# Half of the pairs write their quotient as two float32r parts and multiply w_out in three float32r products; PSUM tiles are handed on in halves

## The chip, the cores and the metric

The kernel runs on one core of a Trainium2 chip. The core has a matrix engine (PE, with its weight loads shown apart as PEld), three engines for elementwise work (DVE, ACT, POOL) and a queue that starts transfers (SP). The metric is the device time of one execution in microseconds; less is better. A time is given as the median of the runs of one kernel, and the traces come from one profiled execution.

## What is computed

A channel attention for four batches, and then a feed-forward layer whose activation is a rational function. Cut to what matters:

```
qn = q / (norm(q, axis=1) + 1e-6)            # q, k, v: 4 x 6080 x 256
kn = k / (norm(k, axis=1) + 1e-6)
s  = kn.transpose(0, 2, 1) @ qn / tau        # 4 x 256 x 256
a  = exp(s - s.max(-1)); a /= a.sum(-1) + 1e-9
x  = (v @ a).reshape(24320, 256)
h  = x @ w_in                                # w_in: 256 x 2048
P  = a0 + a1*h + a2*h^2 + a3*h^3
Q  = 1 + |b0|*|h| + |b1|*h^2
out = (P / (Q + 1e-6)) @ w_out               # w_out: 2048 x 256
```

## The kernel before

**Tiling.** The rows are cut in groups of 512 (the last group of each batch has 448), 12 groups to a batch and 48 in all. The 2048 columns of the hidden layer are cut in eight *pairs* of 2 x 128 columns, so there are 384 units of work, each a pair `p` (0 to 7) of a group. The attention matrix is multiplied into `w_in` once a batch (`fuse`), so that a pair is one product of the value rows with a fused weight. That product is taken in three float32r products of high and low parts: `vhi`, `vlo` and the two halves of a `w` tile (`mm1`, 12 matmuls of 512 columns).

**One pair** (`pair`, L598 to L675). `mm1` writes a tile `hx` of two PSUM banks. Then 1024 values per partition run through the elementwise engines: ACT, DVE and POOL make the denominator `d`. In the plain form ACT squares, POOL multiplies and adds one (`line`), ACT takes the absolute value and POOL adds (`sum`). In the *factored* form (`p` in 1, 3, 6, from the second group on) ACT takes an absolute value, DVE multiplies (`prod`), ACT takes the absolute value again, and POOL adds one (`one`). ACT and DVE make the numerator (`slope`, `num1`, `num2`), which is written over `hx`. ACT takes the reciprocal square root of `d` and squares it, which gives a first reciprocal `r` (`root`, `square`). A Newton step mends it: POOL multiplies `d` by `r` (`again`), DVE forms the quotient with `r` (`quot`) and corrects it into a tile `g` (`last`). `mm2` multiplies `g` by the float32 `w_out_sb` into `acc`, the one accumulator of the group, also two PSUM banks; each of its 8 matmuls stands as two in the trace. After the eight pairs, `finish` copies `acc` to `orow` and stores it.

**Beside the pairs.** While a batch runs, the next batch's scores are gathered (`Attn`: loads of `kq`, squares on ACT, sums `ssq` on POOL, products on PE, `sacc` on DVE). Each weight piece of 512 columns arrives as raw words in a `raw` buffer and is put together by six DVE operations with a `work` tile of its own (`piece`, L302 to L373). Twelve pieces are *early*: their `work` tiles lie in PSUM (`acc` or `hx`). The last four of `w_out` work in the SBUF tiles `cv` and `cv2`.

**What sets the order.** Every operation is a `step` with an engine, a cost and a key. `Planner.order` (L111) runs a list of these steps through a model of the engines, and takes on each engine the ready step with the lowest key whose buffers are free. The keys come from the tables `LAG` and `TIME`. The result is one fixed order per engine; on the chip the engines only wait for each other's semaphores. A buffer tag has a fixed number of slots (`SLOTS`): three `hx` tiles of two PSUM banks, one `acc`, four `d`, four `uu`, three `r`, four `g`.

All operations are recorded by one helper (L43), so the profile is read by tiles and not by lines.

Of the kernel before, what the change touches and what calls it, by code (L numbers as in the profile page):

```python
# [21 lines left out]
    "first": 2.42, "prod": 2.04, "abs": -4.64, "line": 9.56, "second": 3.75, "sum": -23.6, "slope": 5.71,  # L22
    "num1": 23.17, "num2": 21.53, "root": 8.83, "one": -1.7, "square": -3.23, "again": 5.54, "quot": 8.31,
    "last": 10.3, "out": 23.21,
}
TIME = {
    "pair": 3.57, "start": 48.71, "load": 1.9, "softmax": 48.77, "in": 5, "late_in": 3.83, "out0": 2.3,
    "out": 5.39, "attn0_0": -0.02, "attn_0": 0.98, "attn0": 3.82, "attn": 2.42, "attn1": 91.81, "value": 3.3,
    "fuse": 1.77, "finish": 10.12, "front": 45.32, "front_pace": 2.4,
# [20 lines left out]
class Buf:  # L50


    def __init__(self, tag=None, view=None):
        self.tag, self.view = tag, view
        self.tile, self.slot = None, None
        self.writers, self.readers = [], []
        self.left = 0
        self.owner, self.until = None, 0.0

# [8 lines left out]
class Planner:  # L68
# [10 lines left out]
    def add(self, eng, cost, key, fn, reads=(), writes=(), port=False):  # L79
# [20 lines left out]
        for b in {id(b): b for b in (*reads, *writes)}.values():  # L100
            if b.tag is not None:
                b.left += 1
                s.bufs.append(b)
# [7 lines left out]
    def order(self):  # L111
# [17 lines left out]

        def fits(s):  # L130
            want = {}
# [8 lines left out]
        while left:  # L140
            for e in ready:
                while busy[e] <= now and ready[e]:
# [9 lines left out]
                    if pick is None:  # L152
                        break
                    for b in pick.new:
                        b.slot = free[b.tag].pop(0)
# [36 lines left out]
def tile_channel_attention_rational_ffn(  # L192
# [25 lines left out]
    while n0 < N:  # L218
# [8 lines left out]
    FACTORED = (1, 3, 6)  # L227
# [11 lines left out]
    SLOTS = {"hx": 3, "acc": 1, "d": 4, "uu": 4, "r": 3, "g": 4, "w": 10, "kq": 4, "sq": 2, "ssq": 1,  # L239
             "vst": 1, "vhi": 2, "vlo": 2, "orow": 2, "sacc": 1, "eT": 1, "cv": 1, "cv2": 1, "n2": 1,  # L240
             "s0": 1, "y": 1, "e": 1, "sm": 1}
    plan = Planner(SLOTS, ("d", "uu", "r", "g", "w", "kq", "sq", "cv", "cv2", "vst", "vhi", "vlo", "orow", "acc"), ("hx", "acc"))
# [6 lines left out]

    def buf(tag, shape, dtype=F32, name=None):  # L250


        def view(slot):
            sizes = dict(zip("abc", shape[1:]))
            t = homes[tag][slot]
# [6 lines left out]
        homes.setdefault(tag, 0)  # L262
        homes[tag] = max(homes[tag], math.prod(shape[1:]))
        return Buf(tag, view)

    def step(eng, cost, key, fn, reads=(), writes=(), port=False):
# [7 lines left out]
        plan.add(eng, cost, key, run, reads, writes, port)  # L274
# [16 lines left out]
    b0, b1 = babs[:, 0:1], babs[:, 1:2]  # L291
    w_in_sb = const.tile([P, NC2, F], F32, name="w_in_sb")
    w_out_sb = const.tile([P, NF, C], F32, name="w_out_sb")

# [7 lines left out]
    def piece(side, m, at, c):  # L302
# [9 lines left out]
        raw = buf("d" if early else "g", [P, 2 * PIECE], U32, "raw")  # L312
        kept = buf("uu" if early else "cv", [P, 2, PIECE], F32, "kept")
        work = buf(("acc" if side == "in" and m < 4 else "hx") if early else "cv2", [P, 2, PIECE], F32, "work")
# [39 lines left out]
        def cut_off():  # L354
# [3 lines left out]
                dst, keep(), 1.125 * 2.0**-15, unit(F32), op0=ALU.is_ge, op1=ALU.mult  # L358
# [4 lines left out]
        else:  # L363
            dst, ok = w_out_sb[:, 2 * m : 2 * m + 2].rearrange("p f e -> p (f e)"), w_out_ok[m]
# [3 lines left out]
        step("DVE", one, c, low_bits, [raw], [work], port)  # L368
        step("DVE", two, c + 0.1, high_bits, [raw, work], [work], port)
        step("DVE", one, c + 0.2, power, [work], [work], port)  # L370
        step("DVE", two, c + 0.3, low_word, [raw, work, kept], [kept], port)
        step("DVE", two, c + 0.4, together, [work, kept], [work], port)
# [373 lines left out]
```

## Time and profile before

| | |
|---|---|
| time, median of 3 runs | 2692.86 us (2690.3 to 2696.26) |
| profiled execution, first to last instruction | 2694.6 us |
| mean granted TensorE clock | 0.995 |
| HBM traffic | 83.10 MB read, 24.90 MB written |

The profiled execution has no time of its own beside its span. The span lies inside the range of the three runs, so nothing that could be seen lies around it.

The page cuts the span into 40 slices and gives each engine's busy share in tenths:

```profile
PE   7999999999999999999999999999999999999999
DVE  7988888888878778788888878788888888888886
ACT  5778888888788888788878888877887888888885
POOL 6789877877678788877868888877875787787785
```

A 9 is 90% or more. One slice is 67 us; the first one holds the start, in which the first batch's scores are made. Busy time of a group of instructions is the union of their spans; since one instruction's last part may overlap the next one's start, the step from start to start can be shorter than the mean duration.

### The profile page before, as it was taken

To read this page: it belongs to the slowest core of one execution; us is meant where nothing else is said; L and a number is where in the kernel's file an instruction comes from. 1 tells how busy PE (TensorE), PEld (TensorE's weight loads), DVE (VectorE), ACT (ScalarE), POOL (GpSimd) and SP (SyncE) were. 2 spreads that over 40 slices of the span, in tenths; PEclk is the share of its full clock that TensorE was granted. 3 is DMA by queue.
4 is the path that set the end of the run, shared out by engine and by line. 5 is a ranking of instruction groups with operands and counts; after the bars stand their busy time and mean duration, and the time that the engine had idled before them with its cause. 6 is when DMAs were issued, how large, how long until landed. Compare 5 with 4: busy or idle time off the path is not lost.

```text
span 2694.6 us, 32473 instructions
## 1 busy us (share of the span) xinstructions
PE 2653.3 (98%) x12200; PEld 2271.6 (84%) x12200; DVE 2247.6 (83%) x1987; ACT 2195.5 (81%) x2227; POOL 2106.4 (78%) x1104
## 2 busy tenths in 40 slices
PE   7999999999999999999999999999999999999999
PEld 6778888888888888888888888888888888888887
DVE  7988888888878778788888878788888888888886
ACT  5778888888788888788878888877887888888885
POOL 6789877877678788877868888877875787787785
PEclk9999999999999999999999999999999999999999
DMA  9402000000011111100001111100000000000000
GB/s 325 134 32 80 28 16 32 16 18 30 16 31 47 55 55 48 45 32 31 17 16 31 55 55 48 47 30 32 15 16 16 31 16 16 32 16 17 31 9 15
DMA packets 69325, 110.10 MB, mean 41 GB/s; under 512 B 5296, under 2 KB 53936, under 8 KB 69168
## 3 DMA queue, kind: packets, MB, share of 16 engines
q1 hardware_dynamic: 69168, 108.03, 12.3%
q8 instruction: 96, 1.57, 0.2%
q14 instruction: 61, 0.50, 0.1%
HBM read 83.10 MB, written 24.90 MB: 40 GB/s over the span
## 4 chain that ended last, share of the span: by engine, by line
PE 90%; DVE 3%; POOL 1%; issue 1%; ACT 1%; DVEq 0%; POOLq 0%
PE acc L43 47%; PE hx L43 44%; DVE hx L43 1%; POOL d L43 1%; DVE g L43 1%; DVE sq L43 0%; ACT r L43 0%; DVE cv L43 0%; DVE uu L43 0%; DVE y L43 0%; DVE n L43 0%; DVE vlo L43 0%; DVE e L43 0%; ACT d L43 0%; DVE sm L43 0%
## 5 line engine op out<-in xcount | busy, mean ns | idle before, releaser
L43 PE MATMUL acc<-w_out_sb,g 128*128 128x256 f32 (+1 forms) x6144 | 1371.1, 379 | 0.0
L43 PEld LDWEIGHTS acc<-w_out_sb,g 128*128 128x128 f32 (+1 forms) x6144 | 1157.0, 189 | 167.6
L43 POOL TENSOR_TENSOR d<-d,r 128x1024 f32<-128x1024 f32 (+1 forms) x384 | 906.2, 2362 | 187.1 <-ACT r L43 172.9
L43 PE MATMUL hx<-vhi,w 128*128 128x512 f32 (+1 forms) x3072 | 892.5, 401 | 10.4 <-DVE g L43 5.5
L43 PEld LDWEIGHTS hx<-vhi,w 128*128 128x128 f32 x3072 | 579.1, 189 | 125.5 <-ACT sq L43 10.3
L43 DVE TENSOR_TENSOR uu<-uu,hx 128x1024 f32<-128x1024 f32 (+1 forms) x384 | 462.4, 1204 | 189.0 <-ACT uu L43 187.9
L43 POOL TENSOR_TENSOR d<-d,uu 128x1024 f32<-128x1024 f32 (+1 forms) x243 | 573.9, 2362 | 20.3
L43 DVE SCALAR_TENSOR_TENSOR hx<-hx,coef,r 128x1024 f32<-128x1024 f32 (+1 forms) x384 | 490.3, 1279 | 118.1 <-ACT r L43 101.2
L43 DVE SCALAR_TENSOR_TENSOR g<-d,hx 128x1024 f32<-128x1024 f32 (+1 forms) x384 | 463.5, 1207 | 47.2 <-POOL d L43 11.1
L43 DVE SCALAR_TENSOR_TENSOR hx<-uu,coef,hx 128x1024 f32<-128x1024 f32 (+1 forms) x384 | 489.6, 1275 | 7.8
L43 PE MATMUL hx<-vlo,w 128*128 128x512 f32 (+1 forms) x1536 | 474.3, 390 | 0.0
L43 ACT ACTIVATE uu<-hx,coef 128x1024 f32<-128x1024 f32 (+1 forms) x384 | 458.6, 1194 | 0.0
L43 ACT ACTIVATE uu<-hx,babs 128x1024 f32<-128x1024 f32 (+1 forms) x384 | 424.4, 1105 | 26.6 <-PE hx L43 26.6
L43 ACT ACTIVATE r<-d 128x1024 f32<-128x1024 f32 (+1 forms) x384 | 404.1, 1052 | 50.8 <-POOL d L43 46.4
L43 ACT ACTIVATE d<-hx 128x1024 f32<-128x1024 f32 (+1 forms) x243 | 247.0, 1017 | 226.3 <-PE hx L43 226.1
L43 ACT ACTIVATE r<-r 128x1024 f32<-128x1024 f32 (+1 forms) x384 | 403.2, 1050 | 12.1
L43 POOL TENSOR_SCALAR d<-d,babs 128x1024 f32<-128x1024 f32 (+1 forms) x243 | 272.8, 1123 | 166.9 <-ACT d L43 165.8
L43 PEld LDWEIGHTS hx<-vlo,w 128*128 128x128 f32 x1536 | 289.4, 188 | 58.6
L43 POOL TENSOR_SCALAR d<-d,ones 128x1024 f32<-128x1024 f32 (+1 forms) x141 | 157.5, 1117 | 140.9 <-ACT r L43 140.8
L43 ACT ACTIVATE d<-d 128x1024 f32<-128x1024 f32 (+1 forms) x141 | 146.4, 1038 | 57.4 <-DVE d L43 57.4
L43 POOL TENSOR_TENSOR ssq<-sq,ssq 128x1024 f32<-128x1024 f32 (+1 forms) x69 | 165.8, 2403 | 34.8 <-ACT sq L43 33.8
L43 DVE SCALAR_TENSOR_TENSOR d<-uu,babs,hx 128x1024 f32<-128x1024 f32 (+1 forms) x141 | 178.1, 1263 | 13.6 <-ACT uu L43 13.6
(83 smaller groups left out, 1087.3 us busy)
## 6 DMA issues: line engine op xcount, KB each, us to landing
vst<-in_v_dram SPq DMA_DIRECT2D x44, 512.0 KB, 3.5
out_dram<-orow SPq DMA_DIRECT2D x44, 512.0 KB, 2.6
kq<-in_k_dram SPq DMA_DIRECT2D x78, 256.0 KB, 3.7
kq<-in_q_dram SPq DMA_DIRECT2D x78, 256.0 KB, 4.0
d<-in_moe_w_in_dram SPq DMA_DIRECT2D x8, 512.0 KB, 7.0
r<-in_k_dram SPq DMA_DIRECT2D x10, 256.0 KB, 6.6
r<-in_q_dram SPq DMA_DIRECT2D x10, 256.0 KB, 6.6
d<-in_moe_w_out_dram SPq DMA_DIRECT2D x4, 512.0 KB, 7.0
```

The costliest lines, as they stand in the source:

```text
L43: ins = op(*args, **kwargs)
```

## The change

**Kinds of pairs.** From the second group on all eight pairs are factored. The odd ones (`WHOLE`) keep the Newton step and the float32 product; their result goes into `d` instead of `g`. The even ones (`SPLIT`) write the quotient as float32r (`ghi`), multiply it back by `d` on POOL, subtract that from the numerator on DVE in two halves of 512 (the remainder, `rho`), and multiply the remainder by `r` on POOL into a float32r `glo`. In the first group all pairs are plain, and the split ones make `rho` and `glo` on DVE.

**The second product.** A split pair takes `ghi` by `w_out_hi`, `ghi` by `w_out_lo` and `glo` by `w_out_hi`: 24 float32r matmuls of 256 columns in place of 8 float32 ones. The order within `acc` is free after the first.

**Buffers.** `hx` becomes two tags of one bank each, `hx0` and `hx1`, so that a half can be handed on when its own `rho` is done; `mm1` is two steps of six matmuls, one half each. `g`, `cv` and `cv2` go; `ghi` and `glo` have two slots each, `r` four, `w` eight instead of ten, `orow` one instead of two. All `w_out` pieces now work in `r` (SBUF), and four are split in a high and a low part. Costs and keys are new throughout.

```diff
-    "last": 10.3, "out": 23.21,
+    "first": 0.51, "prod": 2.77, "abs": -18.41, "line": -35.04, "second": 2.74, "sum": -14.24,
...
-    FACTORED = (1, 3, 6)
+    KINDS = ['FP', 'FU', 'FP', 'FU', 'FP', 'FU', 'FP', 'FU']
+    FIRST = ['ND', 'ND', 'ND', 'ND', 'ND', 'ND', 'ND', 'ND']
+    SPLIT = [p for p in range(8) if "U" not in KINDS[p]]
+    WHOLE = [p for p in range(8) if p not in SPLIT]
+    RHO2 = 1
...
-        work = buf(("acc" if side == "in" and m < 4 else "hx") if early else "cv2", [P, 2, PIECE], F32, "work")
+        if side == "in" and m >= 4:
+            works = wide([P, 2, PIECE], "work")
+            work = works[0]
+        else:
+            works = work = buf("acc" if side == "in" else "r", [P, 2, PIECE], F32, "work")
...
+        if side == "out" and m in SPLIT:
+            step("DVE", two, c + 0.5, cut_off, [works, kept], [kept], port)
+            hi_ok = Buf()
+            step("ACT", 0.6, c + 0.6, top_part, [kept], [hi_ok])
+            step("DVE", 0.66, c + 0.7, rest, [kept, hi_ok], [ok], True)
...
-        def mm1():
+        def mm1(i):
...
-        step("PE", 2.8 * s, at, mm1, [whi, wlo, vhi, vlo], [hx])
-
-        if m >= NFP and p in FACTORED:
+        for i in range(2):
+            step("PE", 1.365 * s, at + 0.01 * i, lambda i=i: mm1(i), [whi, wlo, vhi, vlo], [hxs[i]])
+
+        if fac:
...
+            fn = lambda: dve.scalar_tensor_tensor(c(ghi), c(hx), a0, c(r), op0=ALU.add, op1=ALU.mult)
+            step("DVE", 1.2 * s, at + lag("quot"), fn, [hxs, r], [ghi])
+            fn = lambda: pool.tensor_tensor(c(d), c(d), c(ghi).bitcast(F32), op=ALU.mult)
+            step("POOL", 2.36 * s, at + lag("again"), fn, [d, ghi], [d])
...
+                    fn = lambda i=i: dve.scalar_tensor_tensor(
+                        half(d, i), half(hx, i), a0, half(d, i), op0=ALU.add, op1=ALU.subtract
+                    )
+                    step("DVE", 0.65 * s, at + lag("rho") + 0.01 * i, fn, [hxs[i], d], [ds[i]])
...
+                fn = lambda: pool.tensor_tensor(c(glo), c(d), c(r), op=ALU.mult)
+                step("POOL", 2.36 * s, at + lag("low"), fn, [d, r, *(ds if RHO2 else ())], [glo])
...
+            hi = ("out", 0.96, ghi, [(ghi, w_out_hi), (ghi, w_out_lo)])
+            lo = ("out_lo", 0.48, glo, [(glo, w_out_hi)])
+            todo = [(*hi, 0), (*hi, 1), (*lo, 0), (*lo, 1)]
```

**DVE in the steady part.** The rows that follow are DVE's before, in a middle group; a name's number is the buffer, `coef` and `babs` are coefficients, and `hx_..<-uu_..,coef` is `num2`, `uu<-uu,hx` is `num1`, `hx<-hx,coef,r` is `quot`, `g<-d,hx` is `last`, `d<-uu,babs,hx` is `prod`.

```order
L43 TENSOR_TENSOR uu_86<-uu_86,hx_90 128x1024
L43 SCALAR_TENSOR_TENSOR hx_90<-uu_86,coef,hx_90 128x1024
L43 SCALAR_TENSOR_TENSOR hx_90<-hx_90,coef,r_109 128x1024
L43 TENSOR_TENSOR uu_85<-uu_85,hx_91 128x1024
L43 SCALAR_TENSOR_TENSOR d_82<-uu_87,babs,hx_92 128x1024
L43 SCALAR_TENSOR_TENSOR g_94<-d_81,hx_90 128x1024
L43 SCALAR_TENSOR_TENSOR hx_91<-uu_85,coef,hx_91 128x1024
L43 SCALAR_TENSOR_TENSOR hx_91<-hx_91,coef,r_107 128x1024
L43 SCALAR_TENSOR_TENSOR g_95<-d_83,hx_91 128x1024
```

The same engine after the change, in a middle group; `ghi<-hx,coef,r` is a split pair's `quot`, and `d<-hx,coef,d` in two halves its `rho`.

```order
L52 SCALAR_TENSOR_TENSOR hx_100<-uu_97,coef,hx_100 128x1024
L52 SCALAR_TENSOR_TENSOR d_92<-uu_96,babs,hx_101 128x1024
L52 SCALAR_TENSOR_TENSOR hx_100<-hx_100,coef,r_104 128x1024
L52 TENSOR_TENSOR uu_98<-uu_98,hx_101 128x1024
L52 SCALAR_TENSOR_TENSOR hx_101<-uu_98,coef,hx_101 128x1024
L52 SCALAR_TENSOR_TENSOR d_91<-uu_95,babs,hx_102 128x1024
L52 SCALAR_TENSOR_TENSOR d_93<-d_93,hx_100 128x1024
L52 SCALAR_TENSOR_TENSOR ghi_144<-hx_101,coef,r_105 128x1024
L52 TENSOR_TENSOR uu_97<-uu_97,hx_102 128x1024
L52 SCALAR_TENSOR_TENSOR hx_102<-uu_97,coef,hx_102 128x1024
L52 SCALAR_TENSOR_TENSOR hx_102<-hx_102,coef,r_106 128x1024
L52 SCALAR_TENSOR_TENSOR d_92<-hx_101,coef,d_92 128x512 x2
```

Every pair now has a `prod`, and the remainder of the pair in `hx_101` stands four rows behind its `ghi`, with other pairs' work between them; before, `prod` came in three pairs of eight.

**PE in the steady part.** Before, a pair's first product went to both halves of an `hx` tile by turns (x2), and the second was one run of float32 matmuls on `g`.

```order
L43 MATMUL hx_91<-vhi_138,w_120 128x512 x2
L43 MATMUL hx_91<-vlo_140,w_120 128x512 x2
L43 MATMUL hx_91<-vhi_138,w_130 128x512 x2
L43 MATMUL acc_89<-w_out_sb,g_94 128x256 x8
L43 MATMUL acc_89<-w_out_sb,g_95 128x256 x8
```

After the change, around the transposes of the next group's values:

```order
L52 MATMUL acc_99<-w_out_hi,ghi_143 128x256
L52 MATMUL acc_99<-w_out_lo,ghi_143 128x256
L52 MATMUL hx_101<-ident,vst_136 128x128 x8
L52 MATMUL acc_99<-w_out_sb,d_92 128x256 x4
L52 MATMUL acc_99<-w_out_hi,glo_145 128x256 x8
L52 MATMUL acc_99<-w_out_sb,d_92 128x256 x4
L52 MATMUL hx_101<-vhi_137,w_120 128x512
L52 MATMUL hx_101<-vlo_139,w_120 128x512
L52 MATMUL hx_101<-vhi_137,w_128 128x512
```

The float32 product of a whole pair is now cut open by a split pair's `glo`, and the halves of `hx` are no longer written by turns.

More of the change, by code (lines that the diff above doesn't have):

```diff
@@ L128, in order, with slots @@
         left = len(self.steps)
+        def slots(s):
+            for b in s.new:
+                rest = free["hx1"]
+                if b.tag == "hx0":
+                    both = any(x.first is b for x in s.new)
+                    ready = [k for k in free["hx0"] if k in rest]
+                    if not ready and not both:
+                        ready = free["hx0"]
+                    return (b, ready[0]) if ready else (b, None)
+                if b.tag == "hx1":
+                    return b, b.first.slot if b.first.slot in rest else None
+            return None, 0
         def fits(s):
+            if slots(s)[1] is None:
+                return False
             want = {}
@@ L593, in values @@
         )
-        step("DVE", 1.2, at + 2, fn, [slot, hi], [lo])
+        step("DVE", 1.2, at + 2, fn, [slots, hi], [lo])
         return hi, lo
@@ L649, in pair @@
+        late_one = fac or "M" in kind
+        more = ONE if late_one else 0.0
         fn = lambda: act.activation(c(r), c(d), AF.Abs_reciprocal_sqrt, bias=more)
-        step("ACT", 1.06 * s, at + LAG["root"], fn, [d], [r])
-        if m >= NFP and p in FACTORED:
+        step("ACT", 0.97 * s, at + lag("root"), fn, [d], [r])
+        if late_one:
             fn = lambda: pool.tensor_scalar(c(d), c(d), ones[:, 0:1], ONE, op0=ALU.mult, op1=ALU.add)
-            step("POOL", 1.13 * s, at + LAG["one"], fn, [d], [d])
@@ L663, in pair @@
-        step("DVE", 1.28 * s, at + LAG["last"], fn, [d, hx], [g])
-        def mm2(i):
-            for t in range(T):
-                pe.matmul(
-                    acc[:pn, t, :], g[:, i, t * pn : (t + 1) * pn], w_out_sb[:, 2 * p + i, :],
-                    start=(p == 0 and i == 0 and t % 2 == 0), stop=(p == NFP - 1 and i == 1),
-                    skip_group_check=True,
-                )
-        for i in range(2):
-            old = [] if p == 0 and i == 0 else [acc]
-            step("PE", 1.72, at + LAG["out"] + 0.1 * i, lambda i=i: mm2(i), [g, w_out_ok[p], *old], [acc])
+            if by_act:
+                fn = lambda: act.activation(c(d), c(d), AF.Identity, bias=ONE)
+                step("ACT", 0.95 * s, at + lag("one"), fn, [d], [d])
+            else:
+                step("POOL", 1.1 * s, at + lag("one"), fn, [d], [d])
@@ new lines, in pair @@
+        for k_, (key, cost, src, parts, i) in enumerate(todo):
+            first = p == 0 and k_ == 0
+            done = Buf()
+            began = [acc] if first else []
+            fn = lambda i=i, parts=parts, first=first: mm2(i, parts, first, True)
+            step(
+                "PE", cost, at + lag(key) + 0.1 * i, fn, [src, w_out_ok[p], *([] if first else acc.began)],
+                [done, *began], uses=[acc],
+            )
+            if first:
+                acc.began, acc.done = [done], []
+            acc.done.append(done)
@@ L680, in finish @@
         orow = buf("orow", [P, T, C])
-        step("ACT", 1.05, at, lambda: act.copy(orow[:pn], acc[:pn]), [acc], [orow])
+        step("ACT", 1.05, at, lambda: act.copy(orow[:pn], acc[:pn]), [acc, *acc.done], [orow])
         row = b * N + base
```

254 lines of the change are left out of this document (178 added, 76 removed).

## The prediction

> **What bounds the kernel now.** I read the page's head first, then its chain that ended last, then the stretches of time, then who waited for whom.
>
> ```profile
> span 2694.6 us, 32473 instructions
> PE 2653.3 (98%) x12200; PEld 2271.6 (84%) x12200; DVE 2247.6 (83%) x1987; ACT 2195.5 (81%) x2227; POOL 2106.4 (78%) x1104
> PE acc L43 47%; PE hx L43 44%; DVE hx L43 1%; POOL d L43 1%; DVE g L43 1%; DVE sq L43 0%; ACT r L43 0%; DVE cv L43 0%; DVE uu L43 0%; DVE y L43 0%; DVE n L43 0%; DVE vlo L43 0%; DVE e L43 0%; ACT d L43 0%; DVE sm L43 0%
> ```
>
> PE is busy for 98% of the span, and 91% of the chain lies on its two products: `acc` (the second) and `hx` (the first, with the smaller ones). The other engines have 450 to 590 us to spare. That is an average, so the stretches come next (columns: stretch, its length, then busy time and count for PE, PEld, DVE, ACT, POOL; granted clock, DMA share, GB/s).
>
> ```profile
> 0.00:60.00 60.00, 47.87 (x198) 39.73 (x199) 43.57 (x60) 32.99 (x36) 40.71 (x24) 0.97 1.01 319
> 60.00:150.00 90.00, 76.59 (x329) 63.10 (x327) 84.42 (x98) 65.55 (x82) 68.30 (x32) 0.94 0.41 131
> 150.00:2640.00 2490.00, 2480.69 (x11450) 2128.27 (x11451) 2090.15 (x1803) 2069.10 (x2082) 1969.90 (x1034) 1.00 0.10 31
> 2640.00:2694.60 54.60, 48.19 (x225) 40.52 (x223) 29.50 (x27) 27.84 (x30) 27.49 (x17) 0.98 0.05 19
> ```
>
> From 150 to 2640 us PE stands for only 9 us. From 60 to 150 us it is DVE that is full (84.4 of 90), and PE waits. DVE's idle time splits in two: 16.4 + 5.6 + 25.1 = 47 us at start and end, and 400 us in the middle. The waits say what the middle part is (engine and tile <- releaser: us in all, times, longest):
>
> ```profile
> DVE uu L43 <- ACT uu L43: 187.9, 130, 4.1
> DVE hx L43 <- ACT r L43: 101.2, 106, 3.1
> ```
>
> These two are most of it, and they cost nothing today because PE hides them.
>
> **The change, part by part.** Durations are of the profiled execution; its span of 2694.6 us is 1.7 us (0.06%) over the median of 2692.86, and I sum against the span.
>
> *PE, the second product.* The timeline shows what a matmul takes from start to start (columns: start, length, engine, operation, count):
>
> ```profile
> 1511.45 1.08 PE L43 MATMUL hx<-vhi,w 128*128 128x512 f32 x4
> 1512.37 0.62 PE L43 MATMUL hx<-vlo,w 128*128 128x512 f32 x2
> 1512.83 0.62 PE L43 MATMUL hx<-vhi,w 128*128 128x512 f32 x2
> 1513.28 1.89 PE L43 MATMUL acc<-w_out_sb,g 128*128 128x256 f32 x8
> 677.02 0.97 PE L43 MATMUL hx<-vhi,w 128*128 128x448 f32 x4
> 677.83 0.57 PE L43 MATMUL hx<-vlo,w 128*128 128x448 f32 x2
> 678.23 0.56 PE L43 MATMUL hx<-vhi,w 128*128 128x448 f32 x2
> 678.63 5.34 PE L43 MATMUL acc<-w_out_sb,g 128*128 128x256 f32 x24
> 2666.84 22.61 PE L43 MATMUL acc<-w_out_sb,g 128*112 128x256 f32 x104
> 52.04 1.04 PE L43 MATMUL hx<-ident,vst 128*128 128x128 f32 x8
> 52.91 3.80 PE L43 MATMUL hx<-r 128*128 128x256 f32 x16
> ```
>
> A float32 product of 256 columns stands as two instructions of 0.216 us (22.61 / 104, less the last one's tail), so a pair's second product takes 16 x 0.216 = 3.46 us. A float32r matmul of 512 columns takes 0.229 us (1513.28 - 1511.45, eight of them), one of 448 columns 0.201 us (678.63 - 677.02, eight). The difference is 0.43 ns a column, and 256 columns fewer than 512 give 0.229 - 0.110 = 0.12 us. No row shows a float32r matmul of 256 columns. From below, eight transposes of 128 columns, each with a weight load, take 0.87 us, 0.109 each; from above, nothing says it is slower than the 448 columns' 0.201. The line through two rows of the same kind is nearest, so I take 0.12. Then 24 x 0.12 = 2.88 us, **0.58 us less for each of 4 x 48 = 192 split pairs: -110 us**. At 0.109 it would be -161 us, at 0.201 it would be +262 us.
>
> The row on the first product also decides a rule of the Trainium skill. "TensorE: Matmul & The Clock Gate", Part 3, section "The mechanism", has weight loads overlap matmuls in flight only where their row groups differ. Here every load fills all 128 rows, so by that rule none is hidden, and with the page's 107 ns for a load of 128 columns (section "LDWEIGHTS (loading the stationary operand)") a 256-column step would be about 0.21 us, an estimate that ends any gain. The trace speaks against it: at 0.43 ns a column the stream alone fills 0.22 of the 0.229 us.
>
> *PE, the rest.* `mm1` keeps 12 matmuls a pair. Writing one half after the other instead of by turns I take at nothing, since the runs on `acc` write the same bank many times in a row at 0.216 us. If PE stayed the bound, the time were 2694.6 - 110 = **2585 us**.
>
> *DVE.* It is the engine that gets work. Steps from start to start, in a stretch without waits:
>
> ```profile
> 1509.04 1.28 DVE L43 SCALAR_TENSOR_TENSOR hx<-hx,coef,r 128x1024 f32<-128x1024 f32 x1
> 1510.24 1.21 DVE L43 TENSOR_TENSOR uu<-uu,hx 128x1024 f32<-128x1024 f32 x1
> 1511.37 1.21 DVE L43 SCALAR_TENSOR_TENSOR g<-d,hx 128x1024 f32<-128x1024 f32 x1
> 1512.50 1.28 DVE L43 SCALAR_TENSOR_TENSOR hx<-uu,coef,hx 128x1024 f32<-128x1024 f32 x1
> L43 DVE TENSOR_TENSOR sacc<-hx,sacc 128x512 f32<-128x512 f32 x28 | 19.3, 688 | 9.8 <-PE hx L43 9.8
> L43 DVE SCALAR_TENSOR_TENSOR d<-uu,babs,hx 128x1024 f32<-128x1024 f32 (+1 forms) x141 | 178.1, 1263 | 13.6 <-ACT uu L43 13.6
> ```
>
> `quot` takes 1.20 us, `num1` 1.13, `last` 1.13; `num2` and `prod` are of `quot`'s kind, 1.20. Half a remainder is like the `sacc` row, 0.69 less the overlap of 0.08 seen here (1.28 against 1.20): 0.61. So a plain pair costs DVE 4.66 us, a factored whole one 5.86, a split one 1.20 + 1.13 + 1.20 + 1.20 + 2 x 0.61 = 5.95. `prod` ran 141 times, 3 x 47, and will run 8 x 47 = 376 times. By place: pairs 0, 2, 4 go from plain to split, 141 x 1.29 = 182 us; pair 6 from factored to split, 47 x 0.09 = 4; pairs 5 and 7 from plain to factored, 94 x 1.20 = 113; the first group's four split pairs get two operations for one, 5; four weight pieces a subtraction more, 3. **Together +307 us.** A remainder without overlap (0.69) adds 30 us, one that is only half of `quot` (0.60) takes 4 away.
>
> *The start.* The early `w_out` pieces worked in PSUM, the late ones in `cv`; now all work in SBUF. Here is one operation of an early piece, and then the same kind in a late piece while POOL runs:
>
> ```profile
> 58.55 0.69 DVE L43 SCALAR_TENSOR_TENSOR uu<-d,hx 128x512 f32<-128x512 uint32 x1
> 79.39 10.72 POOL L43 TENSOR_TENSOR ssq<-sq,ssq 128x1024 f32<-128x1024 f32 x4 [8.61 <-ACT sq L43]
> 79.45 2.85 DVE L43 SCALAR_TENSOR_TENSOR cv<-g,cv 128x512 f32<-128x512 uint32 x1
> 82.33 2.73 DVE L43 TENSOR_TENSOR cv<-cv,cv 128x512 f32<-128x512 f32 x1
> ```
>
> It took 2.85 us in place of 0.69, and the one behind it 2.73. The two are 2.16 + 2.04 = 4.2 us over. With that as a piece's surcharge, the four pieces that move to SBUF cost DVE **+17 us**, in the very stretch where it is full. Bounds are nothing (POOL idle at that moment) and 34 us.
>
> This is the rule of the Trainium skill on "SBUF — State Buffer", section "SBUF: two separate sides": DVE operations with two SBUF inputs and POOL operations that read SBUF lock each other out for a whole instruction. The trace agrees (2.85 us beside POOL's run), and by the rule `prod`, `quot`, `rho` and `last`, which each read one operand from PSUM, stay free of it.
>
> *DVE's sum.* 2247.6 + 307 + 17 = 2572 us busy, and with the 47 us at the ends **2619 us**. Some 30 us of that are tails of 0.08 us before some 400 idle stretches that close up, so the floor is 2590 to 2620. DVE thus reaches and passes PE's 2585.
>
> *ACT and POOL.* ACT keeps five operations a pair; 2195 us are covered. POOL:
>
> ```profile
> L43 POOL TENSOR_TENSOR d<-d,r 128x1024 f32<-128x1024 f32 (+1 forms) x384 | 906.2, 2362 | 187.1 <-ACT r L43 172.9
> L43 POOL TENSOR_SCALAR d<-d,ones 128x1024 f32<-128x1024 f32 (+1 forms) x141 | 157.5, 1117 | 140.9 <-ACT r L43 140.8
> ```
>
> A plain pair cost it 1.12 + 2 x 2.36 = 5.84 us and a factored one 3.48; a split one costs 1.12 + 2 x 2.36 = 5.84, a whole one 3.48. Of 376 pairs 235 were plain and 188 will be split: 47 x 2.36 = 111 us less, 1995 us. That POOL writes float32r is new; I take the same 2.36 us. It has over 600 us to spare, so it becomes a bound only above some 5.5 us each. `orow` with one slot waits for a store once a group, which is hidden behind a group's 56 us.
>
> *The sum.* PE allows 2585 us, DVE 2590 to 2620. With both nearly full, what one waits for the other no longer hides. Today's two DVE waits sum to 289 us; I keep a tenth, about 25 us, on the middle of DVE's floor, 2605, and come to 2630 to 2635: **2632 us**, 2.3% less than now.
>
> **The rivals.**
>
> *PE stays the bound* (2592 us). The fixed order puts every operation where its input is ready, the tails close up, the start costs nothing: 2585 plus a few us of stalls as in the middle today (9 us in 2490). For it speaks that PE lost so little while DVE was at 84%. Against it, DVE would have to run at 98% for 2500 us.
>
> *DVE waits for the remainder's product* (about 2840 us, slower). In a split pair `quot` goes to POOL, 2.36 us, and comes back to DVE as `rho`; only then is `hx` free for a later `mm1`. If DVE reaches `rho` before POOL is done it stands, and all behind it. Half of POOL's operation in each of 188 split pairs is 188 x 1.18 = 222 us on 2619. It turns slower than now from 76 / 188 = 0.40 us for each split pair, a sixth of that operation. For it: DVE has no slack left to hide it. Against it: in the order quoted, three rows of 1.13 us and more lie between `ghi` and its remainder.
>
> *The float32r matmul of 256 columns costs what the load and the stream cost together* (about 2960 us). At the upper end of 0.201 us PE alone needs 2694.6 + 262; from 0.144 us (3.46 / 24) on nothing is gained. Against it stands the line through the two rows. The weight-load rule of the Trainium skill's page on TensorE, cited above, would end here.
>
> *It comes out even.* DVE's waits keep 75 us and eat what PE gains: 2690 to 2698 us.
>
> **How the numbers follow.** The forecast, both engines nearly full (2608 to 2685 us): 0.57. PE stays the bound (2575 to 2608): 0.23. Even: 0.05. DVE waits for the remainder: 0.11. The dear matmul: 0.04. About 0.2%, 5 us, is what a measurement can tell from no change. Faster is 0.57 + 0.23 = 0.80, same 0.05, slower 0.11 + 0.04 = 0.15. The range from 2580 to 2700 leaves out a bit of the second case and both slow ones.
>
> **What would show it.** In the profile after: `acc<-w_out_hi,ghi` matmuls at 0.12 us from start to start (0.2 would mean the third rival); PE busy near 2545 us; DVE busy near 2570 us at 97% or more of the span, `d<-hx,coef,d` near 690 ns, 376 of them; POOL near 2000 us with `glo` at 2.36 us; few waits of DVE `d` for POOL (the second rival has them at hundreds of us); and weight operations of 1 to 3 us on DVE before 150 us. Wrong would be a DVE well below 95% in the middle with PE waiting for `hx`, or PE still at 98%.

## The result and the profile after

The changed kernel takes **2750.86 us** (median of 4 runs, 2750.06 to 2752.46), the kernel before 2694.48 us beside it: a ratio of 1.0217, 95% interval 1.0202 to 1.0231. The change makes the kernel 2.2% slower; the forecast was 2.3% faster. The head of the page after the change, and its chain that ended last:

```profile
span 2750.7 us, 36157 instructions
PE 2599.3 (94%) x13736; PEld 2245.3 (82%) x13736; DVE 2550.4 (93%) x2424; ACT 2231.0 (81%) x2232; POOL 2005.2 (73%) x1057
PE 36%; DVE 33%; ACT 14%; issue 9%; POOL 7%; DMA 0%; SPq 0%; DVEq 0%; POOLq 0%; ACTq 0%
```

Two engines are above 90%, neither reaches 97%, and the chain, 90% PE before when it is summed by engine, now changes engines all the time. Two stretches (length, then busy time and count for PE, PEld, DVE, ACT, POOL; granted clock, DMA share, GB/s) say where DVE's idle time lies:

```profile
60.00:150.00 90.00, 56.90 (x234) 46.79 (x235) 87.99 (x96) 50.05 (x67) 55.49 (x24) 0.81 0.42 131
150.00:2640.00 2490.00, 2394.54 (x12754) 2070.45 (x12752) 2320.39 (x2173) 2063.00 (x2043) 1832.55 (x968) 1.00 0.09 31
```

In the start DVE is full, 88.0 of 90 us, and PE gets to 56.9 us of work where it had 76.6; the granted clock there is 0.81 where it was 0.94, and what that costs no run shows. In the middle DVE lacks 2490 - 2320 = 170 us, so it is at 93%. The waits of the whole run (engine and tile, releaser: us, times, longest):

```profile
PEld hx L52 <- DVE d L52: 153.3, 156, 20.6
PE hx L52 <- DVE d L52: 106.4, 120, 20.2
ACT uu L52 <- PE hx L52: 204.8, 181, 7.0
DVE d L52 <- ACT uu L52: 66.8, 70, 3.3
DVE d L52 <- POOL d L52: 10.9, 22, 1.3
```

PE now stands for `hx` until DVE has read it, ACT stands for `hx` until PE has written it, and DVE's longest wait is that of `prod` for ACT's `uu`: read together, the names go round. DVE hardly waits for POOL.

A view of one tile gives the pace: ACT copies `acc` to `orow` once a group. The row has the count, the duration, and the starts of the first and the last copy; first the kernel before, whole run and a stretch of whole groups of the last batch (which has no score work beside it):

```profile
L43 ACT COPY orow<-acc x48: 994/1015/1021, 178.6 to 2689.5; 128x1024 f32<-128x1024 f32 x44, 112x1024 f32<-112x1024 f32 x4
L43 ACT COPY orow<-acc x6: 1016/1016/1021, 2199.3 to 2451.2; 128x1024 f32<-128x1024 f32 x6
```

The same after the change:

```profile
L52 ACT COPY orow<-acc x48: 991/997/1017, 208.8 to 2745.5; 128x1024 f32<-128x1024 f32 x44, 112x1024 f32<-112x1024 f32 x4
L52 ACT COPY orow<-acc x6: 997/998/999, 2196.2 to 2451.6; 128x1024 f32<-128x1024 f32 x6
```

The first group is 30.2 us late, and from the first copy to the last it takes 2536.7 us against 2510.9, 25.8 us more. A group of the last batch took (2451.2 - 2199.3) / 5 = 50.4 us and takes 51.1.

Against that stands what PE's own steps need. Its timeline in the last batch:

```profile
2302.54 0.28 PE L52 MATMUL acc<-w_out_lo,ghi 128*128 128x256 f32 x1
2302.66 0.40 PE L52 MATMUL hx<-vhi,w 128*128 128x512 f32 x1
...
2305.39 1.12 PE L52 MATMUL acc<-w_out_hi,glo 128*128 128x256 f32 x8
2306.35 3.62 PE L52 MATMUL acc<-w_out_sb,d 128*128 128x256 f32 x16
```

A float32r step of 256 columns takes 0.12 us, as forecast (2302.54 to 2302.66; 8 in 0.96). Four split pairs of 12 x 0.229 + 24 x 0.12 = 5.63 us, four whole ones of 2.75 + 3.46 = 6.21 and eight transposes, 0.87, are **48.2 us a group**: PE needs 2.3 us less than before and takes 0.7 us more. (Before, eight pairs of 6.21 us and the transposes, about 50.5 us of steps, made the 50.4 us.)

DVE in the same stretch:

```profile
2302.39 1.28 DVE L52 SCALAR_TENSOR_TENSOR d<-uu,babs,hx 128x1024 f32<-128x1024 f32 x1
2303.58 1.28 DVE L52 SCALAR_TENSOR_TENSOR hx<-uu,coef,hx 128x1024 f32<-128x1024 f32 x1
2304.97 1.28 DVE L52 SCALAR_TENSOR_TENSOR ghi<-hx,coef,r 128x1024 fp32r<-128x1024 f32 x1
2306.17 1.21 DVE L52 TENSOR_TENSOR uu<-uu,hx 128x1024 f32<-128x1024 f32 x1
2307.42 1.29 DVE L52 SCALAR_TENSOR_TENSOR hx<-uu,coef,hx 128x1024 f32<-128x1024 f32 x1
2308.61 1.28 DVE L52 SCALAR_TENSOR_TENSOR d<-uu,babs,hx 128x1024 f32<-128x1024 f32 x1
2309.81 0.75 DVE L52 SCALAR_TENSOR_TENSOR d<-hx,coef,d 128x512 f32<-128x512 f32 x1
2310.47 1.28 DVE L52 SCALAR_TENSOR_TENSOR hx<-hx,coef,r 128x1024 f32<-128x1024 f32 x1
2312.35 0.75 DVE L52 SCALAR_TENSOR_TENSOR d<-hx,coef,d 128x512 f32<-128x512 f32 x1 [0.59 <-PE hx L52]
```

It is full: in eight groups of this batch its waits for other engines are about 5 us, where they were 45.7 before. And its steps are longer than the forecast's. `prod` to `num2` takes 1.19 us, but `num2` to the `ghi` that reads its result 1.39, and `num1` to its `num2` 1.25 where it took 1.13 between steps that need nothing of each other. The forecast's pairs make 4 x 5.86 + 4 x 5.95 + 1.13 (`vlo`) = 48.4 us a group; it takes 51.1. (`vlo` is DVE's low part of the next values, one step a group.)

### The profile page after: what moved, and what is told of

Its sections match the earlier page's. It is cut to its first block, busy times and chain, and to the rows that moved or that the text cites. A ratio compares the mean times of both kernels' runs of the same rounds, so it can differ in the third digit from the quotient of the medians.

```text
span 2750.7 us, 36157 instructions
## 1 busy us (share of the span) xinstructions
PE 2599.3 (94%) x13736; PEld 2245.3 (82%) x13736; DVE 2550.4 (93%) x2424; ACT 2231.0 (81%) x2232; POOL 2005.2 (73%) x1057
## 4 chain that ended last, share of the span: by engine, by line
PE 36%; DVE 33%; ACT 14%; issue 9%; POOL 7%; DMA 0%; SPq 0%; DVEq 0%; POOLq 0%; ACTq 0%
PE hx L52 22%; PE acc L52 14%; DVE d L52 13%; DVE hx L52 7%; ACT uu L52 6%; POOL d L52 6%; DVE uu L52 6%; ACT r L52 4%; ACT d L52 3%; DVE ghi L52 2%; DVE r L52 1%; DVE vlo L52 1%; POOL orow L52 1%; ACT sq L52 1%; DVE e L52 0%
## 5 line engine op out<-in xcount | busy, mean ns | idle before, releaser
L52 PE MATMUL acc<-w_out_sb,d 128*128 128x256 f32 (+1 forms) x3072 | 706.0, 379 | 2.4 <-DVE d L52 2.4
L52 PEld LDWEIGHTS acc<-w_out_sb,d 128*128 128x128 f32 (+1 forms) x3072 | 565.0, 189 | 76.2 <-DVE d L52 2.6
L52 POOL TENSOR_TENSOR d<-d,ghi 128x1024 f32<-128x1024 f32 (+1 forms) x192 | 454.4, 2367 | 222.4 <-DVE ghi L52 217.3
L52 DVE SCALAR_TENSOR_TENSOR d<-uu,babs,hx 128x1024 f32<-128x1024 f32 (+1 forms) x376 | 475.1, 1264 | 68.6 <-ACT uu L52 66.8
L52 POOL TENSOR_TENSOR glo<-d,r 128x1024 fp32r<-128x1024 f32 (+1 forms) x188 | 447.7, 2381 | 48.8 <-DVE d L52 44.9
L52 POOL TENSOR_TENSOR d<-d,r 128x1024 f32<-128x1024 f32 (+1 forms) x192 | 457.3, 2382 | 18.9 <-ACT r L52 3.7
L52 PE MATMUL acc<-w_out_hi,ghi 128*128 128x256 f32 (+1 forms) x1536 | 394.3, 293 | 2.0 <-ACT orow L52 2.0
L52 PE MATMUL acc<-w_out_lo,ghi 128*128 128x256 f32 (+1 forms) x1536 | 378.0, 282 | 0.0
L52 PEld LDWEIGHTS acc<-w_out_hi,ghi 128*128 128x128 f32 (+1 forms) x1536 | 287.8, 187 | 12.4 <-ACT orow L52 4.6
L52 PEld LDWEIGHTS acc<-w_out_lo,ghi 128*128 128x128 f32 (+1 forms) x1536 | 287.9, 187 | 7.8
```

The costliest lines, as they stand in the source:

```text
L52: ins = op(*args, **kwargs)
```

## The experiments

"After" and "before" mean the two kernels; where an experiment keeps the order, every engine's instructions stand as after the change. The kernel before ran beside each, at 2691 to 2696 us. The last batch is where the pace of a group is read, since no score work stands beside it.

**One part of the change alone: `prod` in every pair, in the kernel before.**

```diff
-    FACTORED = (1, 3, 6)
+    FACTORED = (0, 1, 2, 3, 4, 5, 6, 7)
```

> The kernel before with all eight pairs factored from the second group on, and nothing else: float32 second products, no remainder, its own keys, order made anew. DVE has 235 x 1.2 = 282 us more (to about 2530), POOL 235 x 2.36 = 555 us less, PE the same 2653 us. Theory 'PE and DVE both nearly full wait for each other': slower than before although PE has not more to do, 2730 to 2830 us. Rival 'it is the remainder and its round trip to POOL': PE stays the bound, 2690 to 2710 us.

2719.91 us, ratio 1.0093 (1.0057 to 1.0128). Its engines and its copies of `acc`:

```profile
PE 2658.5 (98%) x12200; PEld 2266.1 (83%) x12200; DVE 2502.5 (92%) x2222; ACT 2213.6 (81%) x2227; POOL 1561.8 (57%) x869
L43 ACT COPY orow<-acc x48: 989/1007/1017, 174.9 to 2712.8; 128x1024 f32<-128x1024 f32 x44, 112x1024 f32<-112x1024 f32 x4
L43 ACT COPY orow<-acc x7: 989/992/1017, 2164.4 to 2472.1; 128x1024 f32<-128x1024 f32 x7
```

This lies between the two expectations. There is no float32r and no remainder, and yet it takes 2537.9 us from the first copy to the last (after: 2536.7) and 51.3 us a group. So this part alone can lose the 26 us that the change loses behind the first group, and what PE wins by float32r does not show on top. That the two numbers agree is not proof of one cause: here PE still has 50.5 us of steps in a group and carries 84% of the chain, and the planner made this order anew with keys that were fitted to three factored pairs.

**DVE's new work cut down, the order kept.** In two kernels `prod` takes a half, or a quarter, of its values.

```diff
-  dve.scalar_tensor_tensor(c(d), c(kk), b0, c(hx), ...)
+  dve.scalar_tensor_tensor(d[:, :, : n // 4], kk[:, :, : n // 4], b0, hx[:, :, : n // 4], ...)
```

The half:

> The changed kernel with the same order on every engine; DVE's prod covers only half of its columns in all 376 factored pairs, so the denominator is wrong in the other half. DVE has 376 x 0.55 = 207 us less. 'DVE is full': the time falls until PE is the bound, to 2590 to 2640 us. 'The round trip holds hx': the chain of each pair is 0.55 us shorter, 376 x 0.55 / 3 = 69 us, near 2682 us. If PE bounds the kernel: no change.

The quarter:

> The kernel after the change in the same order; prod takes a quarter of its 1024 values (three quarters are left out), all of PE's work stays. DVE's busy time falls by about 376 x 0.85 = 320 us to some 2230 us, what it was before the change. Theory A, PE is right behind DVE: the half prod already brought a batch-3 group to PE's 50.5 us, so this brings little more, 2670 to 2700 us. Rival C, the gain of 110 us on PE is there to be had as soon as DVE has its old slack: 2590 to 2640 us, a batch-3 group at 48.5 us. Rival B, the chain through hx: each prod lies on it, so the step is as large as that of the half prod again, 2655 to 2665 us.

2704.26 us for the half (ratio 1.0038, 1.0022 to 1.0054), 2699.47 for the quarter (1.0020, 1.0011 to 1.0030). The quarter's profile:

```profile
PE 2584.5 (96%) x13736; PEld 2248.6 (83%) x13736; DVE 2281.1 (85%) x2424; ACT 2227.7 (83%) x2232; POOL 2004.8 (74%) x1057
L52 ACT COPY orow<-acc x48: 992/997/1017, 208.7 to 2694.3; 128x1024 f32<-128x1024 f32 x44, 112x1024 f32<-112x1024 f32 x4
L52 ACT COPY orow<-acc x7: 995/997/998, 2153.5 to 2456.1; 128x1024 f32<-128x1024 f32 x7
```

The half lies outside all that was expected of it, 2590 to 2640 us with DVE as the only bound and near 2682 with the round trip; the quarter agrees with "PE is right behind DVE". The first 176 us off DVE give 47 us, the next 93 give 5: the wall of 51.1 us a group was DVE, and a second one stands right behind, at 50.4. That one is neither engine's load alone, since PE's own steps are 48.2 us and DVE is at 85%. From 2160 to 2600 us PE and its weight loads still stand for `hx`:

```profile
PE hx L52 <- DVE d L52: 9.6, 17, 0.6
PEld hx L52 <- DVE d L52: 19.9, 28, 1.0
```

With DVE at its old load the kernel is back at the old time, though PE has 110 us less to do. But two things cancel there. From the first copy to the last it takes 2694.3 - 208.7 = 2485.6 us, 25 less than the 2510.9 before, and the first copy comes 30 us late. Those 25 us come from the first three batches, which have score work beside them; in the last batch a group takes 50.4 us, as before.

**PE's work cut down, alone and together with DVE's.** The matmuls of `glo` are not issued.

```diff
   fn = lambda i=i, parts=parts, first=first: mm2(i, parts, first, True)
+  if key == "out_lo":
+      fn = lambda: None
```

Alone:

> The changed kernel with the same order; the 192 third products (glo by w_out_hi, 8 matmuls of 0.12 us each) are left out, so that part of the result is missing. PE has 184 us less. 'DVE is full': the last batch keeps its pace of 51.1 us a group, and the whole falls by at most 40 us, 2710 to 2750. If PE bounds the kernel: near 2567 us. The rival on hx says nothing of PE beyond that: as with DVE full.

With the half `prod`:

> The kernel after the change in the same order, with two parts left out at once: prod takes half of its 1024 values, and the matmuls of glo are not issued. Alone the first gave 2704 us (DVE's busy time down by 176 us, the time by 47), the second 2757 us (PE's work down by 184 us, the time up by 6). Theory A, DVE is full in the groups without attention work and PE, with what it loses standing for hx, is right behind it (51.1 us a group against 50.5): then PE's cut, worth nothing alone, is worth something once DVE is cut, and the time falls below 2704 by 20 to 80 us, to 2625 to 2685 us, a batch-3 group to 47 to 49.5 us. Rival B, neither engine but the fixed order's chain through hx holds the pace: then the second cut stays worthless and the time is 2700 to 2712 us, a batch-3 group 50.5 us.

Alone 2757.25 us: 192 x 8 x 0.12 = 184 us less for PE, and 6 us *more* than after the change, beyond the 2710 to 2750 us that were expected with DVE full. Together 2659.89 us (ratio 0.988, 0.986 to 0.990), and a group takes 49.0 us, both within theory A:

```profile
PE 29%; ACT 26%; DVE 25%; POOL 12%; issue 7%; DMA 0%; SPq 0%; DVEq 0%; POOLq 0%; ACTq 0%
L52 ACT COPY orow<-acc x7: 996/1000/1000, 2174.2 to 2468.0; 128x1024 f32<-128x1024 f32 x7
```

So after a cut of DVE the same cut of PE that was worth nothing is worth 44 us. Both loads count, and neither alone sets the pace. At 49.0 us neither engine is quite full (PE's own steps are 44.4 us; from 2174 to 2468 us DVE is busy for 275 of 294), and the chain passes between four engines; what holds that pace was not tested.

**The float32r products alone, in the kernel before.**

```diff
-    w_out_sb = const.tile([P, NF, C], F32, name="w_out_sb")
+    w_out_sb = const.tile([P, NF // 2, C], F32, name="w_out_sb")
+    w_out_hi = const.tile([P, NF // 2, C], F32R, name="w_out_hi")
...
+            times = 1 if p % 2 else 3
```

An even pair takes `g` (float32r) by `w_out_hi` three times; `w` has nine slots instead of ten.

> The kernel before the change, with its own kinds of pairs and no remainder; only the second product of the even pairs is changed: three float32r matmuls of g by a float32r w_out in place of the float32 one (the low parts are left out, the high product is taken three times, so PE's work is that of the change and DVE, ACT and POOL have what they had before). Late raw words have a buffer of their own and w nine slots; the order is otherwise the old one. If the float32r products are worth what the forecast took, 4 x 48 x 0.58 = 110 us on an engine that is 98% busy, the time is 2590 to 2615 us. If they are not (their steps stretch beside other work, or the order holds the pace anyway), 2670 to 2700 us.

2645.59 us, ratio 0.9819 (0.9804 to 0.9835): 48 us of the 192 x 0.58 = 110 that the matmuls save, between the two expectations.

```profile
PE 2578.1 (97%) x13736; PEld 2239.7 (85%) x13736; DVE 2238.2 (85%) x1987; ACT 2194.0 (83%) x2227; POOL 2113.9 (80%) x1104
PE 46%; POOL 22%; ACT 13%; DVE 10%; issue 6%; DMA 1%; SPq 0%; DVEq 0%; POOLq 0%; ACTq 0%
PEld hx L43 <- DVE g L43: 62.4, 125, 1.7
L43 ACT COPY orow<-acc x7: 1007/1008/1013, 2161.1 to 2457.7; 128x1024 f32<-128x1024 f32 x7
```

A group takes 49.4 us, 1.0 less than before, where PE's steps are 2.3 shorter: PE's share of the chain, 90% before, is 46%, and the loads for `hx` wait for `last` to let go of it. With DVE at 85%, PE's next wait is already one for the elementwise engines to be done with an `hx` tile. Beside the quarter `prod`, which has the same matmuls and 43 us more on DVE, a group is 1.0 us shorter (49.4 against 50.4) and the first copy 27.5 us earlier: that is a rough measure of what the split pairs' way and its start cost where DVE's load is nearly equal.

**The remainder's way through POOL.** `again` of a split pair, between `ghi` and `rho`, takes half its values; alone, and on top of the quarter `prod`.

```diff
-  pool.tensor_tensor(c(d), c(d), c(ghi).bitcast(F32), op=ALU.mult)
+  pool.tensor_tensor(d[:, :, : n // 2], d[:, :, : n // 2], ghi[:, :, : n // 2].bitcast(F32), op=ALU.mult)
```

> The changed kernel with the same order on every engine; POOL's product of d and ghi in the 188 split pairs covers only half of its columns, so the remainder is wrong in the other half. POOL has about 220 us less, and the way from ghi to the remainder is about 1.2 us shorter; DVE and PE do the same work. Theory 'DVE is full' (its steps, with what one waits for the one before it, fill the time): 2735 to 2752 us, at most 0.5% below the changed kernel's 2750.9. Rival 'the remainder's round trip holds hx' (three tiles, 192 pairs with 1.2 us less each, 192 x 1.2 / 3 = 77 us): near 2675 us.

> The run with prod at a quarter (2699 us, a batch-3 group 50.5 us, PE's own steps 48.2 us), and POOL's product of d by ghi at half width too (work left out in both); the same order. If PE stands for hx because the remainder's way through POOL holds it, that way is 1.18 us shorter in 188 pairs: 2640 to 2675 us, a batch-3 group near 49 us. If PE stands for another reason (the order in which it takes the products, hx held by the rest of the chain), nothing comes of it: 2690 to 2702 us, as with DVE full, where it gave 7 us.

2743.86 us (7 less than after, as expected with DVE full) and 2689.11 us (10 less than the quarter alone, just below the 2690 to 2702 us for "another reason"). A group of the last batch stays at 51.1 and at 50.5 us. As the order stands, that way is worth 7 to 10 us and is not what holds the pace.

**The same work, DVE's order loosened.** Where a step stands right behind the one that it reads from, it goes behind the next one, if nothing in between needs it.

```diff
-    steps = plan.order()
...
+    steps = apart(plan.order())
```

> The kernel after the change with all of its work; only the order on DVE is changed behind the planner: where a step stands right behind the one whose result it reads, it is put behind the next step instead, if nothing in between needs it. Such neighbours fall from 514 to 171. In the profile a step behind the one it needs starts 0.12 to 0.2 us later than one that needs nothing (num2 behind num1 1.25 us against 1.13, ghi behind num2 1.39 against 1.20). Theory A, DVE is full and these gaps are what its pair costs more than forecast: 343 of them at 0.13 to 0.19 us are 45 to 65 us of DVE's time, of which the time gets a third to all, since PE is right behind (50.5 us a group): 2690 to 2735 us, a batch-3 group 50.3 to 50.6 us. Rival B, DVE's own order does not hold the pace, or the steps put back delay PE as much as is won: 2742 to 2765 us, a batch-3 group 51 us.

**2962.64 us**, ratio 1.0993 (1.0975 to 1.1012): neither expectation. The gaps went, as the timeline shows (`prod` to `quot` to `num1` to `last` at 1.18 to 1.20 and 1.13 us):

```profile
2461.10 1.27 DVE L52 SCALAR_TENSOR_TENSOR d<-uu,babs,hx 128x1024 f32<-128x1024 f32 x1
2462.28 1.29 DVE L52 SCALAR_TENSOR_TENSOR hx<-hx,coef,r 128x1024 f32<-128x1024 f32 x1
2463.48 1.21 DVE L52 TENSOR_TENSOR uu<-uu,hx 128x1024 f32<-128x1024 f32 x1
2464.61 1.22 DVE L52 SCALAR_TENSOR_TENSOR d<-d,hx 128x1024 f32<-128x1024 f32 x1
```

What came in their place stands in the waits of the whole run:

```profile
POOL d L52 <- DVE ghi L52: 440.3, 164, 5.9
DVE d L52 <- POOL d L52: 127.2, 148, 2.1
```

`ghi` comes one step later, POOL begins `again` later, and `rho` waits for it: 127 us where it was 11. `prod` waits for ACT's `uu` longer too, 143 us where it was 67. In this order a step of 1.2 us on DVE is more room than the pairs' ways have, and this shift costs more than the gaps did. That no order could save the gaps is not shown: the keys were not fitted to the shifted one.

**The start.** The four early `w_out` pieces work in PSUM again; alone, and on top of the quarter `prod`.

```diff
-        if side == "in" and m >= 4:
+        if side == "in" and m >= 4 or side == "out" and early:
             works = wide([P, 2, PIECE], "work")
```

> The changed kernel, but the four early w_out pieces work in hx (PSUM) as before the change; the order is made anew. The first group's result leaves at 208.8 us now and left at 178.6 before. Theory 'weight operations with two SBUF operands wait for POOL in the full start': the first group leaves 10 to 20 us earlier and the whole falls by as much, 2730 to 2742 us. Rival 'the start is longer for the two further operations in the first group and for the keys': within 6 us of 2751.

> The run with prod at a quarter (work left out), and the four early w_out pieces work in PSUM again, as before the change; the same order elsewhere. With DVE full this brought the first group 16 us forward and the end nothing. If the lost time of the start is lost for good once DVE is no longer full, the first group comes out near 193 us in place of 209, and the time is 2680 to 2690 us. If the rest of batch 0 is set by something else (the loads and score work of the next batch), the time stays at 2695 to 2702 us.

2750.95 and 2696.31 us: 0 and 3 us for the end, as the second of the two expectations had it each time. The first group does come earlier (the kernel without the quarter, whole run):

```profile
L52 ACT COPY orow<-acc x48: 991/997/1017, 193.0 to 2743.1; 128x1024 f32<-128x1024 f32 x44, 112x1024 f32<-112x1024 f32 x4
```

16 us of the first group's 30 are the pieces in SBUF; by the end of the batch they are lost again, with DVE full or not. What holds that batch was not found; it ends at 807.6 us after the change and ended at 776.1 before.

**Three kernels whose order the planner made anew** (two pairs in an unfactored form; DVE's results released 0.07 us later in the planner; `rho` in one step).

> The changed kernel, but the split pairs 2 and 6 (94 of 384) make the denominator with one more ACT and POOL operation in place of DVE's prod (square scaled by the root of b1, plus the absolute value, added on POOL); nothing is left out, the order is made anew. DVE has 94 x 1.2 = 113 us less, POOL 94 x 2.36 = 222 us more (to about 2230), PE the same. Theory 'PE and DVE are both nearly full and wait for each other through the three hx tiles': with DVE 2.3 us a group below PE the last batch falls from 51.1 to about 49 us a group, the others by about 2, so 2640 to 2680 us. Rival 'DVE's load does not matter, the length of a pair's chain does' (the chain of these pairs is as long as before): 2735 to 2755.

> The changed kernel, but the planner lets a DVE step that needs the DVE step right before it start 0.07 us later, so that it puts another pair's operation between them where one is ready; the work is the same, the order is made anew. In the last batch a num2 takes 1.34 us from start to start in the mean where 1.20 would do, since quot stands right behind it in most pairs. Theory 'DVE is full, and adjacent dependent steps are part of it': 0.15 us less in most pairs, 384 x 0.15 = 58 us at most, 2690 to 2735. Rival 'these short gaps lie in time in which DVE would wait anyway': within 10 us of 2751.

> The changed kernel with the remainder as one DVE operation of 1024 in place of two of 512; nothing is left out, the order is made anew. Two halves take 1.32 us, one whole 1.20: 188 x 0.12 = 23 us less on DVE, but the first half of hx is handed on 0.66 us later. Theory 'both are full': 2725 to 2745 us. Rival 'handing on halves early is what keeps PE going': slower than 2751, up to 2790.

2890.54, 2863.46 and 2806.67 us: outside every range that was expected. DVE has no more work in them than after the change (98 us less in the first, which puts 215 us more on POOL), and they lose 56 to 140 us. The likely reason is that the keys belong to one set of operations, and so the totals say nothing on the parts that were to be tested. The same holds for the run with `prod` in every pair, whose order was made anew as well. But one stretch of the last of the three does speak, six copies of its last batch:

```profile
L52 ACT COPY orow<-acc x6: 997/998/998, 2462.2 to 2712.9; 128x1024 f32<-128x1024 f32 x6
```

They stand 50.1 us apart, where it was 51.1, with all of the work and as many steps behind the one that they read. `rho` in one step takes 4 x 0.12 = 0.5 us a group off DVE; the other half of that 1.0 us comes with the order. So 51.1 us is no floor of this work; that order loses its time in the batches before.

**The parts made where there is slack.** In the kernel before, with all its work, DVE finishes the quotient into `g` as ever; ACT copies `g` into a float32r `ghi`, POOL subtracts it into `glo`. This for pair 3, and for pairs 3 and 6, with keys fitted again.

```diff
+  if split:
+      step("ACT", ..., lambda: act.activation(c(ghi), c(g), AF.Copy), [g], [ghi])
+      fn = lambda: pool.tensor_tensor(c(glo), c(g), c(ghi).bitcast(F32), op=ALU.subtract)
+      step("POOL", ..., fn, [g, ghi], [glo])
```

> The kernel before the change with all of its work, one pair (p = 3) in two float32r parts: the quotient is finished as before into g; ACT copies g into a float32r ghi, POOL subtracts that from g into a float32r glo, and PE takes the three float32r products. DVE gets nothing but one subtraction for the weight piece, hx is free as early as before. The keys are fitted again by the planner's own model. PE's work falls by 48 x 0.58 = 28 us, ACT's grows by 48 x 1 us, POOL's by 48 x 2.4 = 115 us, to about 2220 us. Theory A, the saving on PE counts where nothing is put on DVE, at about half as in the run with the float32r products alone: 2672 to 2686 us. Rival B, any longer way from g to acc or POOL's load eats it: 2690 to 2720 us.

> The same with two pairs (p = 3 and 6). PE's work falls by 56 us, ACT's grows by 96 us, POOL's by 230 us to about 2335 us, 87% of the span. Theory A: 2650 to 2680 us. Rival B, POOL is now what DVE was in the change, an engine near full whose products PE waits for: 2690 to 2740 us.

2672.60 us (ratio 0.9923, 0.9910 to 0.9937) and 2675.01 us (0.9933, 0.9921 to 0.9946): **both are faster than either kernel**, by less than 1% of the one before. Both lie in the range of theory A. The first one's profile:

```profile
PE 2626.3 (98%) x12584; PEld 2262.2 (85%) x12584; DVE 2244.5 (84%) x1988; ACT 2242.8 (84%) x2276; POOL 2219.3 (83%) x1152
PE 85%; DVE 6%; ACT 3%; POOL 2%; DMA 2%; issue 2%; SPq 0%; DVEq 0%; ACTq 0%; POOLq 0%
L43 ACT COPY orow<-acc x7: 1008/1008/1017, 2186.4 to 2485.7; 128x1024 f32<-128x1024 f32 x7
```

PE still carries 85% of the chain, and a group takes 49.9 us: of the 0.58 us saved, 0.5 appear. The second pair brings a group to 49.2 us, but nothing to the total; POOL is at 87% there. From the first copy to the last it does take 2483.9 us instead of 2491.4, but the first copy comes at 186.6 us instead of 175.6. How much of the 21 us the new keys gave without the pair was not tried.

## Why the prediction was wrong

*What bounds the kernel before* was read right: where DVE was left as it was, a cut on PE paid, 48 us for four pairs, and 21 us for one, with an unknown share of the new keys in it.

*PE's term* was right in size (0.12 us a step, 48.2 us a group) and wrong in worth. In the old order it is worth 48 us of 110. In the change it is worth nothing as long as DVE has its whole load, since a further 184 us off PE gave none, and 25 us behind the first group once DVE is at its old load. PE's busy time hides this: it was to fall to 2545 us and shows 2599. In the last batch its own steps fill 48.2 of 51.1 us, 94%, and from 2200 to 2600 us it shows as busy for 387 of 400 us, 97%; so short waits lie under the tails of its matmuls. The weight-load rule of the Trainium skill, "TensorE: Matmul & The Clock Gate", Part 3, section "The mechanism", by which the prediction estimated a step of about 0.21 us, does not hold for these loads as it was read there: a step takes 0.12 us. The same section also lets a load go ahead into the background weight buffer, and these rows fit that.

*DVE's sum* was right as busy time: 2550 us against 2572. **The step that failed is the next one, that DVE could be driven to 97 or 98% of the span and lose only 25 us to waits, a tenth of today's 289.** The forecast left DVE 2632 - 2572 = 60 us without work, 47 of them at the two ends; it has 2750.7 - 2550.4 = 200, and 170 of them lie in the middle. There it is at 93% with PE waiting for `hx`, which is the sign of being wrong that the prediction named. In the middle its waits sum to 134 us, half of that `prod` waiting for ACT's `uu`.

In the last batch the loss has another form, and there it can be added up. The term itself was taken from start to start in a stretch whose neighbours need nothing of each other. After the change nine of a group's 45 steps stand behind the one they read, 0.12 to 0.2 us longer each, 1.5 us in all; eight half remainders take 0.66 us instead of 0.61, 0.4 us; and one wait of 0.6 to 0.7 us remains. Together that is some 2.6 of the 2.7 us between 48.4 and 51.1. The order before had more such neighbours, 13 a group in this batch, where PE hid them; the few rows that the forecast took its steps from held none. Carried over 47 groups, 2.7 us are 127 us, and 2632 + 127 = 2759, near the 2751 measured. That this sum comes so close is luck: it counts the forecast's waits beside the gaps, and in the batches with score work the loss is of the other kind.

*The floor of the two engines.* The forecast took the larger of two sums, 2585 and 2605, and a small surcharge. The four runs on `prod` and `glo` show how it adds up instead: 2751 with both loads, 2704 and 2757 with one of them cut, 2660 with both. The waits read as if each engine waited, between three `hx` tiles, for what the other is late with; no run takes the ring of tiles apart from the order, so that this stays a reading.

*The start* was right in busy time (the forecast's 17 and 3 us; summed over the tiles of the `w_out` pieces, DVE takes 65 us for them where it took 48). The first group is 30 us late, more than half of the 56 us that the change loses, and the forecast had 17 us of DVE's work there and no term for such a delay. What it is worth at the end stays open, since the early pieces gave 16 us of it back and the end got 0 and 3.

*The rivals.* PE as the bound: refuted. The dear matmul: refuted by 0.12 us. It comes out even: no, DVE's waits kept more than that. DVE waiting for the remainder's product: 10.9 us, refuted for this order, but it is one of the waits that the loosened order ran into. What spoke against it, the three rows between `ghi` and its remainder, fits that. The rival that was missing is the plain one: that `prod` in every pair nearly fills DVE by itself, and what the two engines then cost each other. Alone, with its order made anew, it made the kernel before 24 us slower than the one that ran beside it.

## What to carry to other kernels

A saving on the bound engine is worth at most the distance to the next wall; work that wall out per unit of the steady loop, with the steps' real spacing where each reads the one before, and not from a sum of busy times. Where two engines share a short ring of buffers, cut each alone and then both before believing in one bound. Read the start apart from the steady part: a late first group can hide a gain behind it. And work that a saving needs belongs on the engines with slack and behind the point where the shared buffer is let go: one pair done so, with keys fitted to it, gave 21 us, where four pairs that held `hx` for it lost 56. And where a fixed order is made anew, fit its keys again before its time is compared: three runs here lost 56 to 140 us without that.

## What the runs showed of the hardware

*A DVE step that reads the result of the step before it starts 0.12 to 0.2 us later* than one that doesn't (1.25 against 1.13, 1.39 against 1.19 us, rows above), while steps that need nothing overlap by 0.08 us. The Trainium skill, "VectorE: DVE Perf Modes", section "The DRAIN you can't avoid", has it from eight `tensor_copy` operations that a semaphore after each of them costs nothing extra. For the operations of this kernel, where one waits for the result ahead of it and the other does not, the rows show a difference.

*POOL slows DVE operations with one SBUF input too.* The start after the change, DVE and then POOL:

```profile
76.08 0.43 DVE L52 TENSOR_SCALAR r<-r 128x512 uint32<-128x512 uint32 x1
...
79.36 2.73 DVE L52 SCALAR_TENSOR_TENSOR r<-d,r 128x512 uint32<-128x512 uint32 x1
82.13 2.46 DVE L52 TENSOR_SCALAR r<-r 128x512 uint32<-128x512 uint32 x1
```

```profile
79.14 7.66 POOL L52 TENSOR_TENSOR ssq<-sq,ssq 128x1024 f32<-128x1024 f32 x3 [17.50 <-ACT sq L52]
```

While POOL runs, 79.14 to 86.80 us, `r<-r`, one input and all in SBUF, takes 2.46 us instead of 0.43. The prediction spoke of two inputs only; the same section of the Trainium skill, "SBUF — State Buffer", "SBUF: two separate sides", also names operations in a mode of two ports, and these rows fit that.
